# A gated recurrence with a softmax mixture layer behind it: order of the first loads, of a few sums, and of one group's queries

## The chip, the cores and the metric

The kernel runs on one core of a Trainium2 chip. A core has five engines that run side by side, each with its own queue of instructions: TensorE (PE in the profile; its weight loads are PEld), VectorE (DVE), ScalarE (ACT), GpSimd (POOL) and SyncE (SP), which here only issues transfers. They wait for each other through semaphores. Sixteen DMA engines move data between the chip's memory (HBM) and the core's own memory (SBUF); TensorE writes into a second small memory of banks (PSUM). The metric is the device time of one execution in microseconds (us); lower is better.

## What is computed

The inputs are q, k, v and alpha, float32 of shape (4 batches, 8 heads, 768 tokens, 48), and the weights w_in (384 x 1024), w_out (1024 x 384), which are float64, and a gain g_ln (1024).

```python
for t in range(S):                       # per batch and head
    state = alpha[:, :, t, :, None] * state + einsum('bhd,bhe->bhde', k[:, :, t], v[:, :, t])
    y[:, :, t] = einsum('bhd,bhde->bhe', q[:, :, t], state)
x = y.transpose(0, 2, 1, 3).reshape(B * S, H * D)          # 3072 x 384
h = x @ w_in                                               # 3072 x 1024
e = exp(h - max(h)); sm = e / (sum(e) + 1e-9)              # by row
solu = h * sm
ln = (solu - mean(solu)) / sqrt(var(solu) + 1e-6) * g_ln
out = ln @ w_out                                           # 3072 x 384
```

## The kernel before

**Groups.** The 768 tokens are cut into six groups of 128. A group holds those 128 tokens of all four batches, so 512 rows of the second part. The recurrence over a group is done in one piece, by cumulative products of alpha: keys are divided and queries multiplied by these products, scores between all pairs of tokens are taken on TensorE, masked to the lower triangle, and multiplied with v; a state is carried from group to group.

**Stages of a group's recurrence.** alpha, k and q must stand turned, with the 48 features of a head along partitions and tokens along the free side. The features of a head are split into 32 ("firsts") and 16 ("lasts"), so there are 12 blocks of 32 rows for 8 heads, held as three tiles of four blocks. Group 0 is turned on TensorE by multiplying with the identity (`turned`); later groups on DVE in part (`firsts`, `lasts`) or on TensorE. `scan_back` runs a product scan from the end of the group on DVE (L204), `inverses` and `scan_on` one from its beginning. Then k is multiplied into `kT`, q into `qv` (firsts) and `qe` (lasts). `apart` is a pair of ACT copies (L245) that spread `qe` over blocks, with `parity` deciding which rows are zero. `scores(g, half)` is 64 small matmuls (L278) for four heads: first those over the firsts of every head, then those over the lasts, which read what `apart` wrote. `masked` multiplies scores by the mask on DVE (L289), `read_values` multiplies them with v (L333), and y becomes x.

**Stages of the second part.** For each of eight column blocks `up` computes h = x w_in (L394), ACT takes the exponential `e` (L408), DVE multiplies h by e into `room` (L409), ACT squares that into `u` (L412), and running sums `p` over the column blocks are kept by DVE or POOL (L427). After that `down(n, half)` multiplies a batch's 128 rows by w_out (L507). The layer norm is applied after that product, by `finish(n)`, from sums over columns; `token_sums(g)` turns those sums so that they stand by token: a transpose into `cols` (L467) and three small DVE instructions, a copy into `sums` (L469), a square `sq` (L471) and `s` (L473). `finish` reads `s` and computes the row's scale on DVE, POOL and ACT.

**The weights.** w_in and w_out come as eight pieces of 64-bit numbers (`fetch`, L578), four of w_in (each 256 columns, three requests of 128 rows) and four of w_out; pieces 2 and 3 of w_in are fetched by the same three requests. Five DVE instructions a piece (`bits`) make float32 of them.

**Order.** The order of all instructions on each engine is written out by hand in the program's text. Group g's `up` is interleaved with group g+1's recurrence and group g-1's `down` by a plan: a table says for each of the eight column blocks what of the next group's recurrence is done ahead of it or behind it. Group 1 has a plan of its own (`first`), in which group 2's recurrence has lasts and firsts of the queries behind block 2, `apart` behind block 3, scores behind blocks 4 and 5. `firsts` transposes all eight heads in one DVE instruction (L179); POOL then multiplies them by the products of alpha in two instructions (`queries(0)` and `queries(1)`, L253).

**The start.** SP issues, in this order, alpha (two requests of two batches each), k, q, v and w_in; ACT issues the identity, the mask, `parity` and the gain, behind its first table load. Meanwhile TensorE does 14 matmuls of ones (`warm`, L452), then turns alpha, k and q. A transfer's completion is counted by one of eight semaphores in rotation, and a request waits until the one before it on its semaphore has landed.

The parts that are touched: `warm` (L449), `token_sums` (L454), the first loads (L667 to L689), the turning of alpha (L699 to L704), the multiplies of the queries with `apart` in them (L721), the order at L817 to L826, and "firsts" in `attend` (L882).

Of the kernel before, what the change touches and what calls it, by code (L numbers as in the profile page):

```python
# [32 lines left out]
def fast_path(ctx, tc, q, k, v, alpha, moe_w_in, moe_w_out, moe_g_ln, out):  # L33
# [105 lines left out]
    def by_token(x):  # L139

        return x.rearrange("p h u d -> p (h u d)").rearrange("p (b h d) -> p b h d", b=B, h=H)

    def load_first(src, dst, g):
        t = slice(g * P, (g + 1) * P)
        for b in range(0, B, 2):
            nc.sync.dma_start(
                out=by_token(dst)[:, b : b + 2].rearrange("p b h d -> p (b h) d"),
                in_=src[b : b + 2, :, t].rearrange("b h p d -> p (b h) d"),
            )

    def ends_of(src, tag=None):

        ends = ring.tile([P, T4], FP, name=tag) if isinstance(tag, str) else lots[tag][:, 0:T4]
        ends = ends.rearrange("p (b d) -> p b d", b=B)
        nc.scalar.copy(out=ends.rearrange("p b (h d) -> p b h d", h=H), in_=by_token(src)[:, :, :, E0:D])
        return ends

    def turned(src, ends, out, blocks=range(NB)):

        x = by_token(src)  # L160
        for j in blocks:
            for b in range(B):
                cols = x[:, b, j, 0:E0] if j < H else ends[:, b, E0 * (j - H) : E0 * (j - H) + E0]
                nc.tensor.matmul(
                    out[j // NP][32 * b : 32 * b + 32, j % NP], lhsT=cols, rhs=ident, start=True, stop=True,
                    tile_position=(0, 32 * b), skip_group_check=True,
                )
# [75 lines left out]
    def apart():  # L243
        for i in range(2):
            nc.scalar.mul(  # L245
                out=qv[:, H : 2 * H, 0:P].rearrange("p (j i) t -> p j i t", i=2)[:, :, i], in_=qe[:, :, 0:P],
                mul=parity[:, i : i + 1],
            )
# [22 lines left out]
    def scores(g, half, a=None):  # L271
        a = a or banks("a", [NP, P])
        for last in range(2):
            for i in (0, 2, 1, 3):
                h = half * NP + i
                kb, qb = (H + h // 2, H + h) if last else (h, h)
                for b in range(B):
                    nc.tensor.matmul(  # L278
                        a[b][:, i], lhsT=kT[quarter(b), kb], rhs=qv[quarter(b), qb, 0:P], start=not last and not i, stop=bool(last),
                        tile_position=(32 * b, 0), skip_group_check=True,  # L280
                    )
        masks[half] = a
# [163 lines left out]
                nc.scalar.copy(out=d["p"][:, i], in_=d["q"][i])  # L446
            d["unit"] = small_ones

    def warm(n, ps=ps_o, tag="o"):  # L449
        t = ps.tile([P, 512], FP, tag=tag, name="warm")  # L450
        for i in range(n):
            nc.tensor.matmul(t[:, 0:P], lhsT=ones, rhs=ones, start=True, stop=True)  # L452

    def token_sums(g):  # L454


        d = gr[g]
        t = ps_a.tile([P, B, 2, 32], FP, tag="a3", name="rows") if g else ps_h.tile([P, B, 2, 32], FP, tag="h", name="rows")
        for b in range(B):
            for r in range(4):  # L460
                c = b * P + 32 * r
                nc.tensor.matmul(
                    t[quarter(r), b], lhsT=d["unit"][:, 0:32], rhs=d["p"][:, :, c : c + 32], start=True, stop=True,
                    tile_position=(0, 32 * r), skip_group_check=True,
                )
        tt = work.tile([P, B, 2, 32], FP, name="cols")
        nc.vector.transpose(out=tt.rearrange("p b i t -> p (b i t)"), in_=t.rearrange("p b i t -> p (b i t)"))  # L467
        s = sums[:, g * B : g * B + B]
        nc.vector.tensor_copy(out=s[:, :, 1:3], in_=tt[:, :, :, 0])  # L469
        sq = small.tile([P, B], FP, name="sq")  # L470
        nc.vector.tensor_tensor(out=sq, in0=s[:, :, 1], in1=s[:, :, 1], op=ALU.mult)  # L471
        d["s"] = small.tile([P, B], FP, name="s")
        nc.vector.scalar_tensor_tensor(  # L473
            out=d["s"], in0=sq, scalar=1e-6 * DFF, in1=s[:, :, 2], op0=ALU.mult, op1=ALU.add
        )

    def last_norm():

# [88 lines left out]
    def fetch(i, slot, n=1):  # L567

        kind, f = pieces[i]
        w = n * F // (2 if kind else KC)  # L570
        raw = room[:, 1536 * slot : 1536 * (slot + n)].bitcast(U32).rearrange("p (c f w) -> p c f w", f=w, w=2)
        if kind:
            parts = [(slice(0, P), c, moe_w_out[(f + c) * P : (f + c + 1) * P, :]) for c in range(2)]
        else:
            parts = [(slice(0, P), c, moe_w_in[c * P : (c + 1) * P, f * P : f * P + w]) for c in range(KC)]
        for rows, c, src in parts:
            if float64:
                nc.sync.dma_start(out=raw[rows, c].rearrange("p f w -> p (f w)"), in_=src.bitcast(U32))  # L578
            else:
                dst = w_out[rows, f + c, 0:DM] if kind else w_in[rows, c, f * P : f * P + w]  # L580
                nc.sync.dma_start(out=dst, in_=src)
        for m in range(n):
            raws[i + m] = raw[:, :, w // n * m : w // n * (m + 1)]
# [81 lines left out]
    def inline(x, name):  # L665
        return nc.inline_tensor(np.ascontiguousarray(x, np.float32), name=name).ap()

    load_first(alpha, an, 0)
    nc.vector.memset(mone, -1.0)
    nc.scalar.activation(out=far[:, 0, 1:2], in_=mone, func=AF.Exp)  # L670
    nc.scalar.dma_start(out=ident, in_=inline(np.eye(P), "ident_c"))
    nc.scalar.dma_start(out=mask, in_=inline(np.triu(np.ones((P, P))), "mask_c"))
    odd = np.arange(P) // E1 % 2
    nc.scalar.dma_start(out=parity, in_=inline(np.stack([1 - odd, odd], 1), "parity_c"))
# [10 lines left out]
    nc.gpsimd.memset(kg, 0.0)  # L685
    load_v(0)
    fetch(0, 3)
    fetch(1, 4)
    fetch(2, 1, 2)  # L689
    nc.vector.memset(ones, 1.0)  # L690
    nc.vector.memset(small_ones, 1.0 / 32)
    nc.vector.memset(mhalf, -0.5)
# [3 lines left out]
        return [pool.tile([P, NP, P], FP, tag=tag, name=f"{name}{i}") for i, (pool, tag) in enumerate(where)]  # L696


    warm(14)  # L699
    t = three("tp_a", [(ps_a, "a0"), (ps_a, "a1"), (ps_a, "a2")])  # L700
    turned(an, ends_of(an, 1), t)
    for i in range(3):
        nc.scalar.copy(out=aT[:, NP * i : NP * i + NP, 1:SW], in_=t[i])  # L703
        scan_back(0, i)  # L704
    t = three("tp_k", [(ps_a, "a3"), (ps_h, "h"), (ps_h, "h")])
# [11 lines left out]
    for i in (0, 2, 1):  # L717
        if i == 1:
            scan_on(0, i)
        part = slice(NP * i, NP * i + NP)  # L720
        nc.vector.tensor_tensor(  # L721
            out=qe[:, :, 0:P] if i == 2 else qv[:, part, 0:P], in0=t[i], in1=aT[:, part, 1:SW], op=ALU.mult
        )
        if i == 2:
            apart()
    scores(0, 0)
    t = [x.tile([P, NP, P], FP, tag=n, name="a_" + n) for x, n in ((ps_h, "h"), (ps_o, "o")) for _ in range(2)]
    scores(0, 1, t)
# [92 lines left out]
    down(2, 1)  # L821
    scores(1, 1)
    masked(1)
    finish(0)
    finish(1)
    finish(2)  # L826
# [36 lines left out]
    def attend(a, what):  # L863

        more = a + 1 < G
        if what == "v":
            load_v(a)
        elif what == "keys":
            keys_T(a)
            keys(a)  # L870
            if more:
                load(k, kn, a + 1)
        elif what[:2] == "on":
            if what == "on2":
                inverses(a)
            scan_on(a, int(what[2]))
        elif what == "lasts":
            lasts(qn, qe[:, :, 0:P])
            ends_of_decay()
            queries(2)  # L880
            move_lasts()
        elif what == "firsts":  # L882
            firsts(qn, qv[:, 0:H, 0:P])
            queries(0)
            queries(1)
            move_firsts()
            if more:
                load(q, qn, a + 1)
        elif what == "apart":
            apart()  # L890
        elif what == "decay":
            decay(a)
        elif what == "keys_back":
            if more:
                keys_back(a)
        elif what[:6] == "scores":
            scores(a, int(what[6]))
        elif what[:6] == "masked":
            masked(int(what[6]))
        elif what == "alpha" and more:  # L900
            alpha_T(a + 1)
            if a > 2:
                attend(a, "over")
        elif what == "over" and more:
            alpha_over(a + 1)
            if a + 2 < G:
                load(alpha, an, a + 2)
        elif what == "back" and more:
            for i in range(3):
                scan_back(a + 1, i)  # L910
        elif what == "begin":
            read_begin()
        elif what[:4] == "read":
            read_state(int(what[4]))
        elif what == "values":
            read_values(a)
        elif what == "kv" and more and a != 4:
            next_state(a)
# [535 lines left out]
```

## Time and profile before

| | |
|---|---|
| time, median of 3 runs | 368.23 us (368.16 to 368.46) |
| the profiled execution's own time | 367.97 us |
| its span, first to last instruction | 366.2 us |
| granted TensorE clock | 1.000 |
| ACT and POOL busy | 146.4 us (40%) and 132.2 us (36%) |
| DMA, packets and bytes | 72871 packets, 36.06 MB |

The profile comes from one execution. A row of its timeline gives the start and the busy time (both us), the engine, the line, the operation with output and inputs, the tile shapes, how many instructions were put together in the row, and in brackets how long the engine was idle ahead of it and who released it. A row of the waits view gives engine, name and line that waited, who it waited for, and the total, the number and the longest of these waits. PEld rows are weight loads, which run beside matmuls.

The whole span in 40 slices of 9.2 us, each digit the busy share in tenths (9 is 90% or more):

```profile
PE   8899999999999999999999999999999999999994
DVE  0999989979998797936675935766946314345420
DMA  9995995326196409463035354004041000000011
```

The TensorE row is full from the third slice on. DVE is nearly full from the second slice to the sixteenth or so. The DMA engines are full for the first three slices.

### The profile page before, as it was taken

Reading aid. Unit: us, or ns where it says so; the run is one execution under the profiler, and the core shown is the slowest. Engines: PE = TensorE matmul, PEld = TensorE weight load, DVE = VectorE, ACT = ScalarE, POOL = GpSimd, SP = SyncE. Lnnn points to the kernel's source line nnn. Section 1 sums busy time; section 2 is a strip of 40 time slices with the busy share of each in tenths; the row PEclk is TensorE's granted clock in tenths of the full one; section 3 lists DMA queues with packets and bytes.
Section 4 is the critical chain, followed back from the end, with each engine's and each line's share of the span. In section 5 each row is a group of like instructions: output and inputs, shape, how many; then the busy total and the mean of one; then the engine's idle time right before and its main releaser. Section 6 shows DMA issues by size and latency. Waiting matters only on the chain. (4 is left out here: it accounts for less than half of the span.)

```text
span 366.2 us, 10036 instructions
## 1 busy us (share of the span) xinstructions
PE 357.8 (98%) x4341; PEld 215.0 (59%) x4341; DVE 245.0 (67%) x375; ACT 146.4 (40%) x260; POOL 132.2 (36%) x129
## 2 busy tenths in 40 slices
PE   8899999999999999999999999999999999999994
PEld 8784355666755566566575456475556565555552
DVE  0999989979998797936675935766946314345420
ACT  3647878182645262252521252431241132222110
POOL 7020000004449963774133764232773121233300
PEclk9999999999999999999999999999999999999999
DMA  9995995326196409463035354004041000000011
GB/s 180 183 338 152 204 309 124 88 67 159 50 234 141 109 21 180 85 152 94 21 92 112 83 121 126 3 25 88 21 107 55 0 25 0 24 21 22 23 47 51
DMA packets 72871, 36.06 MB, mean 98 GB/s; under 512 B 48232, under 2 KB 70000, under 8 KB 72816
## 3 DMA queue, kind: packets, MB, share of 16 engines
q1 hardware_dynamic: 71792, 34.39, 39.8%
q10 hardware_dynamic: 1024, 0.92, 0.8%
q8 instruction: 36, 0.59, 0.7%
q14 instruction: 19, 0.16, 0.2%
HBM read 25.30 MB, written 4.72 MB: 82 GB/s over the span
## 5 line engine op out<-in xcount | busy, mean ns | idle before, releaser
L507 PE MATMUL o<-w_out,room 128*128 128x385 f32 x384 | 134.0, 492 | 0.0
L394 PE MATMUL h<-x,w_in 128*128 128x512 f32 x288 | 131.7, 597 | 0.5 <-DVE g_col L642 0.5
L507 PEld LDWEIGHTS o<-w_out,room 128*128 128x128 f32 x384 | 71.0, 189 | 54.7 <-issue 13.1
L394 PEld LDWEIGHTS h<-x,w_in 128*128 128x128 f32 x288 | 53.2, 189 | 58.6 <-issue 48.5
L409 DVE TENSOR_TENSOR room<-h,e 128x512 f32<-128x512 f32 x40 | 27.5, 689 | 72.9 <-ACT e L408 72.9
L408 ACT ACTIVATE e<-h 128x512 f32<-128x512 f32 x40 | 24.0, 599 | 100.2 <-PE h L394 100.2
L427 POOL TENSOR_TENSOR p<-p,e 128x512 f32<-128x512 f32 x30 | 43.7, 1458 | 20.0 <-ACT e L408 19.9
L412 ACT ACTIVATE u<-room 128x512 f32<-128x512 f32 x40 | 25.2, 630 | 38.3 <-DVE room L409 38.3
L546 POOL TENSOR_TENSOR r<-sums,mhalf 128x1 f32<-128x1 f32 x20 | 14.8, 741 | 69.7 <-DVE sums L537 69.4
L289 DVE TENSOR_TENSOR sT<-a,mask 128x512 f32<-128x512 f32 x43 | 26.7, 681 | 8.0 <-PE a L278 7.9
L204 DVE TENSOR_TENSOR_SCAN hT<-aT,unit 128x516 f32<-128x516 f32 x18 | 24.4, 1399 | 7.6 <-ACT aT L703 7.5
L204 DVE TENSOR_TENSOR_SCAN aT<-aT,seed 128x516 f32<-128x516 f32 x18 | 27.4, 1551 | 0.2
L225 POOL TENSOR_TENSOR kT<-kT,hT 128x1024 f32<-128x1024 f32 (+1 forms) x8 | 14.2, 1800 | 32.7 <-DVE kT L179 32.7
L427 DVE TENSOR_TENSOR p<-p,u 128x512 f32<-128x512 f32 x30 | 22.5, 749 | 5.1 <-ACT u L412 5.1
L278 PEld LDWEIGHTS a<-qv,kT 32*128 32x128 f32 x704 | 21.4, 186 | 7.0 <-issue 2.6
L278 PE MATMUL a<-qv,kT 32*128 32x128 f32 x704 | 23.9, 278 | 0.4 <-POOL qv L253 0.3
L212 POOL COPY fend<-hT 128x12 f32<-128x12 f32 x6 | 3.1, 509 | 55.9 <-DVE hT L204 55.9
L333 PE MATMUL y<-sT,vn 128*32 128x128 f32 x768 | 22.6, 273 | 0.2 <-DVE sT L289 0.2
L333 PEld LDWEIGHTS y<-sT,vn 128*32 128x32 f32 x768 | 20.7, 110 | 1.6 <-issue 1.0
L196 ACT ACTIVATE sq<-an,mone 128x1536 uint8<-128x1536 f32 x12 | 18.9, 1572 | 0.2
L548 ACT ACTIVATE o_sb<-o,r 128x384 f32<-128x384 f32 x16 | 9.3, 582 | 18.5 <-POOL r L546 18.5
L261 POOL TENSOR_TENSOR state<-state,lot 128x384 f32<-128x384 f32 x10 | 8.8, 903 | 13.1 <-DMA lot<-qv 13.1
(148 smaller groups left out, 374.3 us busy)
## 6 DMA issues: line engine op xcount, KB each, us to landing
vn<-in_v_dram SPq DMA_DIRECT2D x24, 192.0 KB, 4.7
an<-in_alpha_dram SPq DMA_DIRECT2D x20, 192.0 KB, 4.1
out_dram<-o_sb SPq DMA_DIRECT2D x20, 192.0 KB, 1.9
room<-in_moe_w_out_dram SPq DMA_DIRECT2D x8, 384.0 KB, 5.5
kn<-in_k_dram SPq DMA_DIRECT2D x16, 192.0 KB, 5.6
qn<-in_q_dram SPq DMA_DIRECT2D x16, 192.0 KB, 4.1
lot<-qe SPq DMA_DIRECT2D x40, 64.5 KB, 2.1
lot<-qv SPq DMA_DIRECT2D x20, 129.0 KB, 2.4
```

Source lines behind the costliest of these rows:

```text
L196: nc.scalar.activation(out=sq, in_=x, func=AF.Relu, scale=sign, bias=mone, accum_out=over[:, g, i : i + 1])
L204: nc.vector.tensor_tensor_scan(out=o, data0=a, data1=s, initial=1.0, op0=ALU.mult, op1=ALU.add)
L278: nc.tensor.matmul(a[b][:, i], lhsT=kT[quarter(b), kb], rhs=qv[quarter(b), qb, 0:P], start=not last and not i, stop=bool(last), tile_posit ...
L289: nc.vector.tensor_tensor(out=sT[:, b, half * NP : half * NP + NP], in0=a[b], in1=mask[:, None, :].to_broadcast([P, NP, P]), op=ALU.mult,)
L333: nc.tensor.matmul(y_bank(b)[quarter(r), a], lhsT=lhsT, rhs=rhs, start=(b, r) not in begun, stop=stop, tile_position=(row, 32 * r), skip_g ...
L394: nc.tensor.matmul(h, lhsT=w_in[:, a, f * P : (f + 1) * P], rhs=d["x"][:, a].rearrange("p b t -> p (b t)"), start=(a == 0), stop=(a == KC ...
L408: nc.scalar.activation(out=e, in_=h, func=AF.Exp)
L409: nc.vector.tensor_tensor(out=u, in0=h, in1=e, op=ALU.mult)
L412: nc.scalar.activation(out=u2, in_=u, func=AF.Square)
L427: eng.tensor_tensor(out=p, in0=d[0][i] if f == 1 else p, in1=d[f][i], op=ALU.add)
L507: nc.tensor.matmul(d["o"][:, 0 : DM + 1], lhsT=u_of(g, f)[:, b * P : b * P + P], rhs=w_out[:, f], start=(f == 0), stop=(f == FC - 1), skip ...
L546: nc.gpsimd.tensor_tensor(out=r, in0=s[:, 3:4], in1=mhalf, op=ALU.pow)
```

## The change

**Start.** The identity is issued first on ACT. Alpha's first group is fetched by eight requests of 96 KB, heads 0 to 3 of the four batches and then heads 4 to 7, batches 0 and 1 from SP and 2 and 3 from ACT. The table load, mask, `parity` and gain come behind them on ACT. The first 14 warm matmuls are 92 x 92 instead of 128 x 128. TensorE turns alpha's first four blocks, the copy and the scan of that tile are issued, and then come the copy of the ends (`ends_of`, the lasts of all heads) and the other eight blocks.

**Weights.** Six of w_in's nine requests move from the start to the place behind group 0's `apart`. A small ACT copy into the place they write holds them until then.

**Sums.** The three small DVE instructions of `token_sums(0)` move from behind the transpose to just ahead of `finish(0)`.

**Queries.** For group 2 the transpose of the firsts and the multiplies are done in halves: four heads transposed, multiplied by POOL, then the other four.

```diff
-    def warm(n, ps=ps_o, tag="o"):
+    def warm(n, ps=ps_o, tag="o", w=P):
         t = ps.tile([P, 512], FP, tag=tag, name="warm")
         for i in range(n):
-            nc.tensor.matmul(t[:, 0:P], lhsT=ones, rhs=ones, start=True, stop=True)
+            nc.tensor.matmul(t[0:w, 0:w], lhsT=ones[:, 0:w], rhs=ones[:, 0:w], start=True, stop=True)
...
+        def rest():
+            nc.vector.tensor_copy(out=s[:, :, 1:3], in_=tt[:, :, :, 0])
+            sq = small.tile([P, B], FP, name="sq")
+            nc.vector.tensor_tensor(out=sq, in0=s[:, :, 1], in1=s[:, :, 1], op=ALU.mult)
+            d["s"] = small.tile([P, B], FP, name="s")
+            nc.vector.scalar_tensor_tensor(
+                out=d["s"], in0=sq, scalar=1e-6 * DFF, in1=s[:, :, 2], op0=ALU.mult, op1=ALU.add
+            )
+
+        if g:
+            rest()
+        else:
+            d["rest"] = rest
...
-    load_first(alpha, an, 0)
+    nc.scalar.dma_start(out=ident, in_=inline(np.eye(P), "ident_c"))
+    for h in (slice(0, NP), slice(NP, H)):
+        for b in range(B):
+            queue = nc.sync if b < 2 else nc.scalar
+            queue.dma_start(out=by_token(an)[:, b, h], in_=alpha[b, h, 0:P].rearrange("h p d -> p h d"))
     nc.vector.memset(mone, -1.0)
     nc.scalar.activation(out=far[:, 0, 1:2], in_=mone, func=AF.Exp)
-    nc.scalar.dma_start(out=ident, in_=inline(np.eye(P), "ident_c"))
...
     fetch(0, 3)
-    fetch(1, 4)
-    fetch(2, 1, 2)
...
-    warm(14)
+    warm(14, w=92)
     t = three("tp_a", [(ps_a, "a0"), (ps_a, "a1"), (ps_a, "a2")])
-    turned(an, ends_of(an, 1), t)
     for i in range(3):
+        if i == 0:
+            turned(an, None, t, range(NP))
+        elif i == 1:
+            turned(an, ends_of(an, 1), t, range(NP, NB))
         nc.scalar.copy(out=aT[:, NP * i : NP * i + NP, 1:SW], in_=t[i])
         scan_back(0, i)
...
         if i == 2:
             apart()
+            nc.scalar.copy(out=slots[4][:, 0:1], in_=parity[:, 0:1])
+            fetch(1, 4)
+            fetch(2, 1, 2)
...
     masked(1)
+    gr[0]["rest"]()
     finish(0)
...
         elif what == "firsts":
-            firsts(qn, qv[:, 0:H, 0:P])
-            queries(0)
-            queries(1)
+            for i, n in ((0, NP), (NP, NP)) if a == 2 else ((0, H),):
+                firsts(qn[:, i : i + n], qv[:, i : i + n, 0:P])
+                for j in range(i // NP, (i + n) // NP):
+                    queries(j)
             move_firsts()
```

## The prediction

> **What bounds the kernel now.** I read the page's busy times first, then the waits of PE, then the timeline around each wait, engine by engine.
>
> ```profile
> span 366.2 us, 10036 instructions
> PE 357.8 (98%) x4341; PEld 215.0 (59%) x4341; DVE 245.0 (67%) x375; ACT 146.4 (40%) x260; POOL 132.2 (36%) x129
> ```
>
> TensorE is busy for 98% of the span, so a gain must come from one of its few waits. The waits view lists them; these are all that reach 0.2 us.
>
> ```profile
> PE tp_k L164 <- DMA kn<-in_k_dram: 0.9, 1, 0.9
> PE h L394 <- DVE g_col L642: 0.5, 1, 0.5
> PE tp_a L164 <- DMA an<-in_alpha_dram: 0.3, 1, 0.3
> PE a L278 <- POOL qv L253: 0.3, 1, 0.3
> PE y L333 <- DVE sT L289: 0.2, 1, 0.2
> PE tp_q L164 <- DMA qn<-in_q_dram: 0.2, 1, 0.2
> ```
>
> All but the fourth lie before 29 us. The timeline of the start and of the two later places:
>
> ```profile
> 8.64 3.48 DVE L204 TENSOR_TENSOR_SCAN hT<-aT,unit 128x516 f32<-128x516 f32 x3 [7.54 <-ACT aT L703]
> 14.99 0.80 PEld L164 LDWEIGHTS tp_q<-ident,qn 128*32 128x32 f32 x28 [0.47 <-DMA qn<-in_q_dram]
> 17.35 0.68 DVE L721 TENSOR_TENSOR qe<-tp_q,aT 128x512 f32<-128x512 f32 x1
> 18.07 1.34 ACT L245 ACTIVATE qv<-qe,parity 128x512 f32<-128x512 f32 x2 [2.42 <-DVE qe L721]
> ...
> 78.50 1.65 PEld L278 LDWEIGHTS a<-qv,kT 32*128 32x128 f32 x56 [0.34 <-DVE qv L811]
> 80.41 0.69 DVE L289 TENSOR_TENSOR sT<-a,mask 128x512 f32<-128x512 f32 x1 [1.97 <-PE a L278]
> ...
> 109.55 2.05 DVE L179 STREAM_TRANSPOSE qv<-qn 128x1024 f32<-128x1024 f32 x1
> 111.43 0.69 DVE L427 TENSOR_TENSOR p<-p,u 128x512 f32<-128x512 f32 x1
> 111.68 2.44 POOL L253 TENSOR_TENSOR qv<-qv,aT 128x512 f32<-128x512 f32 x2 [0.81 <-DVE qv L179]
> 113.12 2.26 PE L278 MATMUL a<-qv,kT 32*128 32x128 f32 x64 [0.26 <-POOL qv L253]
> 113.28 1.32 ACT L245 ACTIVATE qv<-qe,parity 128x512 f32<-128x512 f32 x2
> 113.41 1.25 DVE L427 TENSOR_TENSOR p<-p,u 128x512 f32<-128x512 f32 x1 [0.69 <-ACT u L412]
> ```
>
> Three stages matter. (1) To 20 us: DVE's first scan waits 7.54 us for alpha, and from there DVE runs almost without a gap to 78.45. (2) At 78 us PE waits about half a microsecond (its previous matmul ends at 77.98, the next weight load of this group is at 78.50) for DVE's last multiply (L811, 77.76 to 78.45), which frees the bank that scores(1,0) writes. (3) At 113 us PE finishes group 1's h at 112.71 and waits to 113.12 for POOL's query multiply. From scores(2,0)'s end at 115.3 I see no PE wait that these edits could touch.
>
> **Two rules of the Trainium skill.** "SBUF — State Buffer", section "SBUF: two separate sides", says that DVE and GpSimd share a port pair as an exclusive lock for a whole instruction, which a DVE operation with two SBUF inputs contends for. The trace agrees: `p` (L427) takes 0.69 us at 111.43, but 1.25 at 113.41, where it ends 0.54 us after POOL's multiply does (114.12). The forecast goes by these rows. "DMA: Bandwidth & Descriptors", section "Issuing engines are not separate DMA queues", says that the queues of SP and ACT share the same 16 engines. Here the 192-byte packets of alpha, k and q moved some 220 KB per us with the DMA engines solidly busy from 2 to 11 us: the trace does not contradict it, so two issuing engines should not bring q in earlier.
>
> **Part 1: identity first, alpha by halves.** Bytes stay the same; 8 requests replace 2. Alpha landed at 4.64 (batches 0,1) and 6.79; heads 0 to 3 of all batches should now land near 4.4. The 14 warm matmuls shrink from 5.11 us to (92/128) of it at best on the columns, 3.7; as the first ones run at the slow rate (0.213 us per record till 4.6, then 0.112), I take their end as 5.2 rather than 6.12. Then 16 turns (half of some 1.8 us), the copy (0.59) and handing over give a first scan at about 7.0 instead of 8.64. Three scans of 1.16 start-to-start need the second alpha half (6.8, then turns and a copy: 8.4), so they end at 10.7 rather than 12.12: DVE 1.4 earlier. But the q transfer, behind the same bytes, still lets PE turn q only at 14.99. The first q tile is ready at 16.0, the third (needed for `qe`) at 16.9. Before, DVE reached `qe` late (17.35) because it was behind; now it waits for PE and starts about 17.0. So of 1.4 us only 0.35 survives. `apart` (1.34, zero idle behind it) follows, then scores(0,0), which needs it for its last half: end 20.02 becomes 19.66. Its own unhindered length, 1.79 from 17.73, would end at 19.52, so the cap is 0.5 unless q itself lands earlier. Masks, y, the w_in conversion and the first h (28.39, after DVE's 28.24) follow on DVE without a gap, so they shift too: **-0.36**. What the trace doesn't show is q's landing under the new order: the eight requests use up the rotating completion semaphores, so k must be issued after a first quarter has landed (about 4.4, while alpha still occupies the engines till 6.8: hidden) and q after a last one. Bounds: +0.3 (k or q held, or a cold clock after a shorter warm-up) to -1.0 (q 0.6 earlier).
>
> **Part 2: six w_in requests behind `apart`.** They move from SP's 17.9 to 21.15 to about 19.1 to 22. SP now waits on an ACT copy of 128 elements (0.2, behind which stands ACT's score copy at 20.33, itself idle 0.92 before). Pieces 1 to 3 landed by 25.5 and 29.54 and are converted from 27.3 and 31.3: some 1.5 us of cover. Piece 0 (landed 23.52, needed 23.91 before, 23.55 now) is ahead in the queue. **0**, between -0.1 and +0.3 if piece 0 or 1 slips.
>
> **Part 3: three DVE instructions later.** `rest` costs start to start 63.16 to 63.65, 0.49. DVE is without a gap from there to 78.45, so scores(1,0)'s bank comes free 0.49 earlier: PE -0.5 at 78.5. At 80.41 DVE waits for PE again, so the chain behind starts 0.5 earlier also. At 88.0 the same 0.49 is put in before finish(0), into a DVE stretch with no idle from 80.41 to 112.7 but 0.34 at 105.08, which comes from DVE's own sums through POOL and ACT and so moves along. PE, 0.5 ahead, meets DVE again at scores(2,0): its last half waits for `apart` (two ACT copies, ends 113.99 and 114.61; PE's next starts at 114.04 and 114.66: no slack), `apart` for `u`, this for DVE's room (ends 112.71), which stands in that chain. So **-0.03**: gained at 78, given back at 115. Bounds -0.5 (idle inside DVE takes it) to +0.5.
>
> **Part 4: third queries by halves.** The transpose's halves take 0.98 start to start, 1.16 each (row of 128x512 at 65.64). POOL's first multiply starts at about 110.8 and, at 1.09 alone, ends at 111.87. That releases PE's wait for it (0.4), but scores(2,0) ends with `apart`, so nothing comes of that. DVE's `p`, due at 111.5, now meets a running POOL instruction; by the row at 113.41 it ends 0.55 after POOL, 112.42 instead of 112.12. room, u, `apart` and the end of scores(2,0) are that much later: **+0.30**. Below: -0.1 (the lock spares it; `apart` gates anyway). Above: +1.4, if POOL's second multiply is let in ahead of `p` (1.09 more); before, the two alternated.
>
> **Sum:** -0.36 + 0 - 0.03 + 0.30 = -0.09 us. The profiled execution took 367.97 (span 366.2 and 1.8 around it), so 367.88; the median is 0.26 above that execution, hence 368.14, said as 368.1.
>
> **Rivals.**
> - *Faster.* q lands earlier because kn and qn are no longer interleaved with mask and gain requests, or DVE after 80 us has more give than I read. Then -0.7 at the start, or -0.5 of stage 2 stays; with +0.3 or 0 at part 4 the sum is -0.6 to -1.3; at its centre 367.3. For: all first-stage waits are for DMA or DVE, and both are relieved. Against: bytes and packet size are unchanged.
> - *Slower: the port lock.* POOL takes both halves before `p`: +1.4 in place of 0.30, sum +1.0, 369.2. It decides from the point where the second transpose half signals POOL (111.69 + 0.1) before the first multiply ends (111.87), which my own figures just allow; against it, the alternation seen before.
> - *The transfers swallow the start.* DVE waits 0.4 for w_out at 49.5. If that stream doesn't move up, DVE alone keeps the old time, and with stage 2's release the PE wait returns as 0.34: sum about +0.3, 368.5, inside "no change".
> - *It doesn't do what it says.* The halves of part 4 aim at the query wait, but `apart` ends the stage; that is in the forecast.
>
> **Numbers.** Measurement can tell about 0.2% (0.74 us) from nothing. Forecast with the third rival 0.43; faster 0.36; slower 0.21 (port lock 0.13, a held k, q or w_in transfer 0.08). The likeliest case's own range is 367.6 to 368.8; with the two sides' centres the range becomes 366.9 to 369.1.
>
> **What would show it.** First scan at 7.0 (8.64); q's turn still at 14.99; scores(0,0)'s end at 19.66; first h at 28.0; no PE wait at 78; `p` near 111.5 lengthened to about 0.9 to 1.1; the end of scores(2,0) at 115.2. Wrong if q lands over 0.4 earlier or later, if the DVE chain from 80 to 112 shows idle that absorbs 0.5, or if `p` waits for two POOL multiplies.

## The result, and the profile after

The changed kernel is slower: 369.63 us median (368.52 to 370.81, 11 runs) against 368.14 us (367.66 to 368.80, 11 runs) of the kernel before in the same set. The ratio is 1.0042 with a 95% interval of 1.0033 to 1.0052, so +1.5 us, outside the forecast range. The single runs also spread twice as far as those of before.

The profiled execution took 368.77 us, one of the faster ones. Page, then TensorE's waits up to 120 us:

```profile
span 367.0 us, 10048 instructions
PE 358.2 (98%) x4341; PEld 214.6 (58%) x4341; DVE 245.6 (67%) x376; ACT 146.2 (40%) x261; POOL 130.8 (36%) x129
```

```profile
PE tp_k L164 <- DMA kn<-in_k_dram: 1.2, 1, 1.2
PE warm L452 <- DVE ones L697: 1.1, 1, 1.1
PE a L278 <- ACT qv L245: 0.7, 1, 0.7
PE y L333 <- issue: 0.3, 1, 0.3
PE y L333 <- DVE sT L289: 0.2, 1, 0.2
```

The waits for POOL's query at 113 us and for `g_col` at 28 us are gone. Two are new: one for `apart` (ACT qv L245), and one with no releaser ("issue"), in which TensorE waits for nothing that the profile shows. The timeline rows that answer to those of before:

```profile
7.80 3.48 DVE L204 TENSOR_TENSOR_SCAN hT<-aT,unit 128x516 f32<-128x516 f32 x3 [6.70 <-ACT aT L713]
14.94 0.80 PEld L164 LDWEIGHTS tp_q<-ident,qn 128*32 128x32 f32 x28 [0.17 <-DMA qn<-in_q_dram]
16.93 0.69 DVE L731 TENSOR_TENSOR qe<-tp_q,aT 128x512 f32<-128x512 f32 x1 [0.18 <-PE tp_q L164]
17.65 1.34 ACT L245 ACTIVATE qv<-qe,parity 128x512 f32<-128x512 f32 x2 [2.06 <-DVE qe L731]
23.34 3.04 PE L333 MATMUL y<-sT,vn 128*32 128x128 f32 x102 [0.26 <-issue]
...
77.78 1.88 PEld L278 LDWEIGHTS a<-qv,kT 32*128 32x128 f32 x64 [0.55 <-DVE qv L824]
...
109.44 2.07 DVE L179 STREAM_TRANSPOSE qv<-qn 128x512 f32<-128x512 f32 x2
111.33 1.04 DVE L427 TENSOR_TENSOR p<-p,u 128x512 f32<-128x512 f32 x1
110.74 2.58 POOL L253 TENSOR_TENSOR qv<-qv,aT 128x512 f32<-128x512 f32 x2
112.39 1.17 PE L278 MATMUL a<-qv,kT 32*128 32x128 f32 x32
114.30 1.34 PE L278 MATMUL a<-qv,kT 32*128 32x128 f32 x32 [0.73 <-ACT qv L245]
```

q is turned at 14.94 and `qe` made at 16.93, as forecast. At 78 us the weight loads run through (64 in one row); before, the group broke at 78.50. At 111 us `p` takes 1.04 us, and scores(2,0), which could start at 112.39, breaks off in its middle until `apart` is done at 114.30.

Set against each other matmul by matmul, the two traces run like this (us, after minus before at the same instruction):

| place | before | after | difference |
|---|---|---|---|
| first h | 28.39 | 27.95 | -0.44 |
| h's third column block starts | 35.31 | 35.22 | -0.09 |
| first matmul behind scores(1,0) | 80.49 | 79.78 | -0.71 |
| scores(2,0) starts | 113.12 | 112.39 | -0.73 |
| first matmul behind scores(2,0) | 115.32 | 115.57 | +0.26 |
| span | 366.2 | 367.0 | +0.8 |

At their own places parts 1, 3 and 4 read as forecast in this trace. The start's gain, however, is gone between 28 and 35 us, where the forecast saw nothing. Behind 115 us another 0.24 is lost in y at 296 us and 0.3 in the last store. This execution lies 0.86 below the median: what the others lose isn't in it.

### The profile page after: what moved, and what is told of

The parts are those of the page before. It is cut to its first block, busy times and chain, and to the rows that moved or that the text cites. A ratio compares the mean times of both kernels' runs of the same rounds, so it can differ in the third digit from the quotient of the medians.

```text
span 367.0 us, 10048 instructions
## 1 busy us (share of the span) xinstructions
PE 358.2 (98%) x4341; PEld 214.6 (58%) x4341; DVE 245.6 (67%) x376; ACT 146.2 (40%) x261; POOL 130.8 (36%) x129
## 5 line engine op out<-in xcount | busy, mean ns | idle before, releaser
L427 POOL TENSOR_TENSOR p<-p,e 128x512 f32<-128x512 f32 x30 | 42.2, 1405 | 20.0 <-ACT e L408 19.9
L427 DVE TENSOR_TENSOR p<-p,u 128x512 f32<-128x512 f32 x30 | 23.7, 790 | 5.2 <-ACT u L412 5.2
L333 PE MATMUL y<-sT,vn 128*32 128x128 f32 x768 | 23.4, 274 | 0.5 <-issue 0.3
L333 PEld LDWEIGHTS y<-sT,vn 128*32 128x32 f32 x768 | 20.9, 110 | 2.4 <-issue 1.7
```

Source lines behind the costliest of these rows:

```text
L333: nc.tensor.matmul(y_bank(b)[quarter(r), a], lhsT=lhsT, rhs=rhs, start=(b, r) not in begun, stop=stop, tile_position=(row, 32 * r), skip_g ...
L427: eng.tensor_tensor(out=p, in0=d[0][i] if f == 1 else p, in1=d[f][i], op=ALU.add)
```

## The experiments

Every set carried the kernel before along; its median was 367.98 to 368.08. Theory A stands for the port pair at 111 us, B for an unsteady start. C (TensorE's instruction supply) came from the first four traces. D is a cost in parts 1 or 3 that no trace had shown, E a wait of TensorE for w_in's data or for a bank.

### One part undone at a time

Each takes one part of the change back to the text of before, all else as changed. For the queries, as an example:

```diff
-            for i, n in ((0, NP), (NP, NP)) if a == 2 else ((0, H),):
+            for i, n in ((0, H),):
```

> Everything of the change but the queries by halves. Theory A (the port pair at 111 us: POOL's second multiply holds back DVE, and the half-way copies and the end of scores(2,0) with it): the loss is gone, 368.0 us, 0.1 below the kernel before, and the runs lie as close together as those of before (about 1 us). Theory B (the start: transfers or TensorE's instruction supply under the new order of requests vary from run to run): still about +1.1 us over before, with runs spread over 2 us.

> Everything but the identity and alpha by halves and the smaller warm-up. Theory A: still slower than before by 1.0 to 1.6 us, since the loss lies at 113 us and what the start gains is mostly spent by then. Theory B: 0 to +0.5 us over before, runs close together.

> Everything but the deferral of six w_in requests. Theory A: as the changed kernel, +1.2 to +1.6 us. Theory B, if the late w_in requests are the disturbance: 0 to +0.5 us; if alpha's are: +1.5 us.

> Everything but the move of the three small DVE instructions. Theories A and B: PE's wait at 78 us is back (0.4 us) but DVE is 0.5 us earlier at 112 us, so the time is that of the changed kernel within 0.3 us, +1.2 to +1.8 over before.

| undone | median (runs) | ratio to before, 95% |
|---|---|---|
| queries by halves | 369.09 (367.68 to 372.47) | 1.0027 (1.0013 to 1.0041) |
| alpha by halves | 369.29 (368.20 to 372.00) | 1.0033 (1.0021 to 1.0046) |
| w_in later | 368.81 (367.94 to 369.74) | 1.0017 (1.0009 to 1.0025) |
| sums later | 368.83 (367.73 to 372.97) | 1.0026 (1.0010 to 1.0042) |

A alone falls: without the halves the kernel stays 1.1 us slower. B's culprit isn't alpha. Without the deferral 0.6 to 0.8 us are left (0 to 0.5 expected under B), so it isn't the deferral alone either. What stands out is the spread: the three kernels that keep the late w_in requests have runs up to 372 and 373, the one without them ends at 369.74. TensorE's waits up to 45 us with the sums undone (this profiled execution took 372.97):

```profile
PE h L394 <- issue: 2.3, 1, 2.3
PE tp_k L164 <- DMA kn<-in_k_dram: 1.6, 1, 1.6
...
PE y L333 <- issue: 0.9, 1, 0.9
...
PE kv L371 <- issue: 0.3, 1, 0.3
```

Three waits "for nothing" add up to 3.5 us. The trace tells what they are. On a queue of their own, transfers of 16,384 bytes run all through the kernel, 36 in each trace:

```profile
q8 instruction: 36, 0.59, 0.7%
```

The breaks stand at TensorE's 961st, 1217th and 1473rd instruction in every one of these traces: 256 apart, so one transfer per block of 256 instructions at 64 bytes each. These are the fetch times from the traces' DMA records, and what TensorE did at the block's edge:

| kernel of the trace | 3rd fetch | goes on | idle there | 4th fetch | goes on | idle there | 5th fetch | goes on | idle there |
|---|---|---|---|---|---|---|---|---|---|
| before | 20.99-21.93 | 23.25 | 0 | 27.46-28.45 | 31.18 | 0 | 32.44-33.36 | 34.88 | 0 |
| changed | 20.91-21.85 | 23.34 | 0.5 | 27.83-28.80 | 30.73 | 0 | 32.31-33.23 | 34.68 | 0.24 |
| w_in undone | 21.15-22.09 | 23.37 | 0.6 | 27.69-28.69 | 30.85 | 0 | 32.53-33.45 | 34.80 | 0.24 |
| alpha undone | 21.80-22.75 | 24.23 | 1.1 | 29.36-30.33 | 31.84 | 0.4 | 34.99-36.05 | 37.49 | 1.9 |
| halves undone | 21.79-22.73 | 24.21 | 1.3 | 29.86-30.84 | 32.27 | 0.7 | 35.27-36.22 | 37.65 | 1.6 |
| sums undone | 21.59-22.53 | 23.94 | 1.2 | 29.43-30.41 | 31.78 | 0.5 | 35.41-36.63 | 37.98 | 2.5 |

(Idle: the gap between two starts less the usual one.) Wherever TensorE waited at an edge it went on 1.28 to 1.51 us after the fetch had ended. In this trace of the kernel before the fifth block came just in time: 1.52 us. In the changed kernel's the start puts TensorE 0.44 ahead and the fetch comes only 0.13 earlier, so TensorE waits again: between these two traces that is where the start's gain went. Fetch times scatter from run to run: in a second trace of the kernel before (below) the fifth began at 30.64 and cost nothing. The 0.24 lost in y at 296 us stands at such an edge too, the 8129th instruction (28 blocks behind the 961st): its fetch ended at 294.88 and it starts 1.3 us later.

In the traces with alpha, halves or sums undone ACT, and in two of them DVE, also waited for w_in's data, by 0.3 to 0.8 us at 24 and 32 us. But near 35 us ACT waits for TensorE's h and DVE for ACT, while TensorE has no releaser.

Why are the fetches late? The view by stretches of time (start and end of the stretch, its length, busy time of five engines, clock, DMA share, GB/s), first of the kernel before:

```profile
22.00:26.00 4.00, 3.80 (x130) 3.49 (x128) 3.91 (x7) 2.04 (x4) 1.63 (x3) 1.00 1.01 376
26.00:30.00 4.00, 3.54 (x28) 2.34 (x20) 3.79 (x7) 3.30 (x8) 0.00 (x0) 1.00 0.43 172
```

and with the sums undone:

```profile
22.00:26.00 4.00, 2.86 (x93) 2.44 (x93) 3.20 (x6) 1.29 (x3) 1.33 (x2) 1.00 0.96 254
26.00:30.00 4.00, 4.00 (x53) 2.94 (x45) 3.79 (x6) 3.15 (x7) 0.00 (x0) 1.00 0.72 288
```

The w_in stream has moved: 376 GB/s from 22 to 26 us became 254, and 172 from 26 to 30 became 288. The fourth fetch begins in both near the end of this stream (last packets at 28.35 and 31.35), at 27.46 and at 29.43. The fifth follows 5 to 6 us later; with the sums undone the first of group 1's loads, in 192-byte packets from 33.68 us on, are then ahead of it, and in the microsecond before 35.41 no other data moves. In the kernel before these packets start at 33.00, behind the fifth fetch. This is theory C: the late requests of w_in delay TensorE's instructions. The changed kernel's own trace has nearly the same rates (250 and 284) and its fourth fetch at 27.83, so the fetch can come late when the stream has moved, but need not.

### One part alone

> The kernel before with the deferral of six w_in requests alone. Theory C (the deferred requests bring TensorE's own instruction fetches, which the trace shows as 16 KB transfers, late: TensorE runs out of instructions near 35 us): median +0.6 to +1.3 us over before, single runs up to +4, and in a slow profiled run a TensorE wait without a releaser (issue) of over 1 us between 34 and 38 us. Theory A (only the port pair at 111 us costs): within 0.2 us of before.

> The kernel before with the identity and alpha by halves and the smaller warm-up alone. Theory C: the first h comes 0.4 us earlier than in the kernel before, but near 34.7 us TensorE must wait for the same instruction fetch (its fetch ends near 33.2 us and TensorE goes on some 1.4 us later), so that at 44 us it is level: the time within 0.2 us of before. The forecast's own step: -0.36 us, 367.65.

> Parts 1 and 3 together, w_in's requests and the queries as before. Theories A and C: TensorE reaches 112 us 0.6 to 0.7 us earlier than before and waits that much longer for POOL's queries; the time within 0.2 us of before, runs within 1.2 us of each other. Rival D (a cost in part 1 or 3 that no trace here has shown): +0.4 us or more.

> The kernel before with the queries by halves alone. Theory A: DVE's p near 111.5 us is held by POOL to about 1.0 us instead of 0.69, the end of scores(2,0) comes 0.3 to 0.5 later, time +0.3 to +0.5 us. If A is wrong: -0.3 to 0.

| kernel | median (runs) | ratio to before, 95% |
|---|---|---|
| w_in later alone | 369.84 (367.98 to 372.19) | 1.0049 (1.0025 to 1.0074) |
| alpha by halves alone | 368.13 (367.60 to 370.45) | 1.0007 (0.9995 to 1.0018) |
| alpha and sums | 368.56 (367.67 to 369.37) | 1.0010 (1.0001 to 1.0019) |
| queries by halves alone | 368.44 (367.94 to 369.50) | 1.0012 (1.0006 to 1.0019) |

The deferral alone makes a loss as large as the whole (expected up to +1.3, measured +1.8 in seven runs, interval 0.9 to 2.7). Its profiled execution was its fastest, so the wait of over a microsecond isn't in that trace. Alpha alone brings nothing that can be told: its first h came not 0.4 earlier but 1.4 us later in the profiled run, because the third fetch came at 22.95 and y stood idle for 2.0 us at that block's edge. A wait at an edge was expected, but at the fifth block's.

Alpha and sums cost 0.4, where 0.2 at most was expected: rival D is right that something was missing. The trace (of 369.01 us) shows it:

```profile
PE y L333 <- issue: 1.3, 1, 1.3
PE a L278 <- POOL qv L253: 0.8, 1, 0.8
```

The third fetch came at 22.12, so TensorE reached its first h 0.66 later than in the kernel before, and the wait that the sums take away at 78 us only brought it level (+0.04). The three DVE instructions, done later, then lengthen DVE's way (28.67 us from 80.62 to the `qe` transpose, 28.18 before), and scores(2,0) starts 0.68 later. In this trace, then, part 3 costs: it is neutral only where TensorE isn't late already.

The halves alone cost 0.44, as theory A has it:

```profile
111.39 1.04 DVE L427 TENSOR_TENSOR p<-p,u 128x512 f32<-128x512 f32 x1
112.35 0.68 DVE L409 TENSOR_TENSOR room<-h,e 128x512 f32<-128x512 f32 x1
113.73 1.42 DVE L427 TENSOR_TENSOR p<-p,u 128x512 f32<-128x512 f32 x1 [0.70 <-ACT u L412]
```

`p` takes 1.04 instead of 0.69, as in the changed kernel, and `room` and all behind it shift by 0.33.

### The block edges moved

If instructions run short, then dummy instructions far ahead must matter: 16 fewer warm instructions move every edge 16 instructions later in the work. Each warm matmul counts as four instructions (two loads, two multiplies).

```diff
-    warm(14, w=92)
+    warm(10)
```

The other way it is `warm(18, w=72)`; before_again is the kernel before, unchanged.

> The changed kernel with 10 warm matmuls of 128 x 128 in place of 14 of 92 x 92: 16 TensorE instructions fewer ahead of everything, and about the same time for them. Theory C (instruction supply): every edge between two fetched blocks falls 16 instructions later in the work, which between 34 and 38 us are eight matmuls of 0.43 us; the wait there shrinks from 1.5 to 2.5 us to under 0.7, and the median falls by 0.6 to 1.3 us to 368.3 to 369.0. Rival E (TensorE waits there for w_in data or a bank): no change, 369.0 to 369.9.

> The changed kernel with 18 warm matmuls of 72 x 72: 16 TensorE instructions more ahead of everything, so every edge between fetched blocks falls 16 instructions earlier in the work. Theory C: TensorE meets the edge of its fifth block some 2 us earlier, while the fetch comes no sooner: waits of 2 to 4 us between 31 and 37 us, median 370.3 to 371.8. Rival E: 369.0 to 369.9.

> The kernel before once more, for a second trace of it. Theory C: TensorE goes on at its 961st, 1217th and 1473rd instruction (256 apart, 16 KB of 64 bytes) no earlier than 1.35 us after the end of the third, fourth and fifth instruction fetch, and waits there by less than 0.5 us; time 368.0 within 0.6.

> The kernel before with the identity and alpha by halves alone, and 10 warm matmuls of 128 x 128. Theory C: the edges fall 16 instructions later, so the start's gain of 0.3 to 0.4 us outlasts 44 us: 367.5 to 367.8, faster than before. Rival E: as with 14 of 92 x 92, 368.1.

With 16 instructions fewer the changed kernel falls to 368.53 us (1.0014, 1.0006 to 1.0023), with 16 more it rises to 374.73 (371.01 to 377.91; 1.0141, 1.0105 to 1.0177 without the highest run), for warm matmuls that take 4.63 and 4.37 us (4.60 in the changed kernel). That decides for C against E; the second went beyond what was expected. TensorE's waits of that kernel from 20 to 200 us, those above 0.2:

```profile
PE o L513 <- issue: 1.8, 1, 1.8
PE kv L371 <- issue: 1.5, 1, 1.5
PE a L278 <- ACT qv L245: 0.9, 1, 0.9
PE h L394 <- issue: 0.5, 1, 0.5
```

The fifth edge now falls into kv (the state update behind h's first block), where instructions are short, and a later edge, at its 4545th instruction (14 blocks behind the 961st), costs 1.8 us more near 144 us. With 10 the wait at h is gone; 0.8 us at y stays, as the third edge moved only among y's short matmuls. The second trace of the kernel before has idle time of 0.72 at the third edge too (under 0.5 expected), yet its first h comes at 28.46 (28.39): there DVE's w_in conversion, which ends near 28.2 in both, hides it. It ran 367.92 us, as expected. Alpha alone with 10 warm matmuls gave 368.18 us, 1.0005 (0.9994 to 1.0017; 367.5 to 367.8 expected): lowest run 367.20, but half of the runs above 368.3. No gain is shown. Its trace, of 367.46 us, has the third fetch at 20.27 and no idle time at the edge; alpha alone's, of 369.24 us, had it at 22.95.

Last, the edges moved by 44 instructions, with 3 warm matmuls of 128 x 512:

```diff
-                nc.tensor.matmul(t[0:w, 0:w], lhsT=ones[:, 0:w], rhs=ones[:, 0:w], start=True, stop=True)
+                nc.tensor.matmul(t[:, 0 : P * w].rearrange("p (r c) -> p r c", c=P), lhsT=ones,
+                                 rhs=ones[:, None, :].to_broadcast([P, w, P]), start=True, stop=True)
...
-    warm(14, w=92)
+    warm(3, w=4)
```

> The changed kernel with 3 warm matmuls of 128 x 512 in place of 14 of 92 x 92: about the same time, 44 TensorE instructions fewer, so every edge between fetched blocks falls 44 instructions later in the work (the fifth's near 43 us instead of 34). Theory C: no wait for instructions is left between 20 and 43 us but up to 0.5 us in y; what remains is part 4's cost less the start's gain: 368.0 to 368.4, runs within 1 us of each other. If the deferral costs in another way: 369 or more.

> The identity and alpha by halves alone, with 3 warm matmuls of 128 x 512. Theory C: the start's gain of 0.35 to 0.45 us reaches the end in nearly every run: 367.5 to 367.7, and no second group of runs above 368.3 as with 10 warm matmuls. If the start doesn't gain even with instructions at hand: 368.0 and more.

The changed kernel fell as expected, to 368.40 us (1.0012, 1.0004 to 1.0020; the runs 1.6 us apart where 1 was expected), with no idle time left at the three edges, though its warm-up took 5.49 us. Alpha alone did the opposite of what was expected: 369.15 us (367.72 to 371.57; 1.0029, 1.0017 to 1.0041). Its trace, of the run of 367.83 us, has the third fetch at 22.49 and 1.3 us of idle time in y. In the traces with w_in's requests early the third fetch began anywhere from 20.3 to 23.0 us, in those with the deferral from 20.9 to 21.8, with the two behind it later. Its runs above 369 us have no trace, and what they lose stays open.

### The stage at 113 us

Is it `apart` that ends scores(2,0)? It was moved ahead of the exponential of block 3:

```diff
-        head={3: "keys_back"},
+        head={3: "keys_back apart"},
...
-            0: "v", 1: "on1", 2: "lasts firsts", 3: "apart", 4: "scores0 masked0", 5: "scores1 masked1 decay",
+            0: "v", 1: "on1", 2: "lasts firsts", 4: "scores0 masked0", 5: "scores1 masked1 decay",
```

> The kernel before with group 2's apart issued behind keys_back of block 3 and ahead of that block's exponential on ACT, instead of behind its square. Theory A (the end of scores(2,0) is set by apart, not by the queries): apart ends near 112.2 us instead of 114.6, scores(2,0) starts as before, runs its own 1.8 us and ends 0.3 to 0.4 us earlier: 367.6 to 367.8. If apart does not set it: no change, or +0.3 by the later exponential.

> The same with the queries by halves. Theory A: with apart out of the way the half-way query is what scores(2,0) needs; it starts when TensorE arrives (112.7), ends by 114.6, 0.7 to 0.8 us before the kernel before: 367.2 to 367.5, so part 4 turns from a cost of 0.4 us to a gain of 0.3 over the whole-query kernel. If the port pair itself is the cost: 367.8 to 368.2, no better than with whole queries.

> Parts 1, 3 and 4, w_in's requests as before, 10 warm matmuls of 128 x 128, apart ahead of the exponential. Theories A and C together: start -0.3, 78 us -0.4 (no longer given back, since DVE's chain ends in apart no more), 113 us -0.4: 366.9 to 367.3, below both kernels. If another wait takes the place: 367.6 to 368.0.

> Parts 1 and 3 with 10 warm matmuls of 128 x 128 in place of 14 of 92 x 92. Theory C (edges 16 instructions later): 0.3 to 0.6 us below parts 1 and 3 with 92 x 92, 367.6 to 368.0, with the gain of part 3 still given back at 113 us.

Measured with `apart` early: 368.60 us (1.0019, 1.0008 to 1.0031) with whole queries, 368.12 (1.0005, 0.9997 to 1.0014) with halves, and 368.61 (1.0013, 1.0003 to 1.0023) with parts 1, 3 and 4 and 10 warm matmuls. Parts 1 and 3 with 10 warm matmuls, `apart` as before, gave 368.17 (1.0009, 0.9998 to 1.0019). With 14 the ratio was 1.0010, so the gain of 0.3 to 0.6 us that was expected from the edges isn't shown, though the medians lie 0.4 apart. From the end of scores(1,0) to that of scores(2,0) it was 34.83 us before, 34.76 with the early `apart` alone, 35.24 with halves alone, and 34.36 with both. So with the halves `apart` did end the stage, and with it out of the way they gain. With whole queries its removal brings 0.07 and not the 0.3 to 0.4 expected: POOL's second multiply, which ends at 114.19, holds the weight loads there. And the wait moved on. With `apart` early the exponential and with it the masks come later, and scores(2,1) is what stretches:

```profile
113.08 2.07 PE L278 MATMUL a<-qv,kT 32*128 32x128 f32 x64
115.08 2.84 PE L394 MATMUL h<-x,w_in 128*128 128x512 f32 x6
117.85 2.69 PE L278 MATMUL a<-qv,kT 32*128 32x128 f32 x64
```

In this kernel (halves, `apart` early) the first score group of 64 takes 2.07 and the second 2.69. What was gained at 115 us is lost by 121. The time of the whole-query version is no measure of this stage alone: its trace also has 1.1 us of idle time at the third edge, and that of parts 1, 3 and 4 has 1.6. The expected 366.9 to 367.3 was missed, and so was 367.6 to 368.0, expected if another wait took the place; no version ran clearly below the kernel before.

## Why the prediction was wrong

- **Part 2 failed, and with it the forecast.** "0, between -0.1 and +0.3 if piece 0 or 1 slips" looked only at those who wait for w_in's data. It left out what else is fetched at that time: TensorE's own instructions, whose fourth and fifth blocks came up to 2.4 and 3.0 us later than in the first trace of the kernel before. Deferral alone measured +1.8 us (interval 0.9 to 2.7). The changed kernel loses 0.9 us less with its edges 16 instructions later (+0.55 over its set's median instead of +1.49). How the stream holds up a fetch is not shown. For the data itself the step held in the changed kernel's trace; where pieces slipped, in the traces with parts undone, DVE and ACT waited up to 0.8 us, and TensorE's waits show none for it. The hint was in the trace of before, in 16 KB transfers at 27.46 and 32.44 and TensorE going on 1.52 us after the second; only its named waits were read, and this one was just hidden.
- **Part 1**: -0.36 was right at its place in the changed kernel's trace (-0.44 at the first h; `qe` at 16.93 for 17.0; q at 14.94 for 14.99). The first scan came at 7.80 instead of 7.0, since the warm-up ended at 5.7 and not 5.2; this cost nothing. That the gain would "follow on DVE without a gap" to the end was wrong: TensorE met an instruction block that came hardly sooner. Where w_in's requests stay early even the gain at the first h is not sure: alone, part 1 showed none (1.0007, 0.9995 to 1.0018).
- **Part 3**: right for the changed kernel's trace. Gained 0.62 at 78 us for 0.5; DVE's way from 80 to its `qe` transpose at 108.6 grew from 28.18 to 28.62 us, 0.44 for 0.49; given back at 115. That it needs TensorE on time at 78 us was not seen.
- **Part 4**: right in mechanism and size. `p` 1.04 (0.9 to 1.1), cost +0.36 in the trace (DVE's `room` ahead of it stood at -0.10, the end of scores(2,0) at +0.26) and +0.44 (0.2 to 0.7) alone, for +0.30. POOL's second multiply was not let in first. Here the Trainium skill's rule agrees with the trace: "SBUF — State Buffer", "SBUF: two separate sides", has the pair locked for a whole instruction, and `p` ended 0.54 us after POOL's first multiply (111.83), while POOL's second took 1.54 us instead of 1.09.
- **The slower rival** stood on the wrong mechanism: the port lock cost 0.4, not 1.4; that its centre of 369.2 lies near the measured time is luck. In the numbers: of +1.5 us, 0.9 goes away with the edges and 0.4 is part 4; the last 0.2 is not assigned.
- **Two readings of the trace of before** were off and cost nothing: the list of TensorE's waits leaves out 1.1 us ahead of the first warm matmul, and w_in's pieces 1 and 2 are first read at 28.23 and 31.73, not at 27.3 and 31.3, so their cover was larger than written.

## What to carry to other kernels

A transfer's cost is not only when its data is needed but what else is being fetched then, an engine's own instructions included. Where an engine runs hundreds of short instructions while big loads stream, look at the instruction fetches, and at how closely the engine follows them. Waits marked "issue" a fixed number of instructions apart (256 here) point to such a shortage, and dummy instructions added or removed far ahead test it. Before halving a step to start its consumer earlier, find what ends that consumer.

## What the runs showed of the hardware

TensorE's instructions come in 16 KB blocks of 256 while it runs: 36 transfers in each of the twenty traces. One took 0.9 to 2.7 us (in the traces of the kernel before 0.9 to 1.7). In traces with the deferral the fourth began at 27.8 to 29.9 us, without it at 26.8 to 28.2; the fifth at 32.3 to 35.4 with it, and at 30.4 to 34.2 without. When a fetch is asked for is not in the trace, so how long it was queued can't be told.

A shortage can cost a second time. With the sums undone, TensorE's break near 36 us was followed by a stretch at half clock (the view by stretches as above, the clock third from the end):

```profile
36.00:39.00 3.00, 1.02 (x3) 0.54 (x4) 0.66 (x1) 0.28 (x1) 0.00 (x0) 1.00 0.85 160
39.00:43.00 4.00, 4.00 (x7) 1.68 (x6) 2.42 (x3) 1.72 (x5) 0.00 (x0) 0.57 0.92 197
43.00:47.00 4.00, 4.00 (x10) 1.71 (x9) 3.31 (x5) 3.88 (x8) 0.00 (x0) 1.00 0.65 147
```

It lasted 3.41 us, during which a matmul of h took 0.85 us from start to start instead of 0.43, by estimate about 1.7 us lost. With 18 warm matmuls the same came after the break near 144 us. The Trainium skill's "TensorE: Matmul & The Clock Gate", "Part 1: The HAM clock gate", gives windows of some 3.4 us after which an idle TensorE falls to half rate. The stretch has that length, but the breaks ahead of it were shorter than a window (2.9 us from one start to the next here, 2.3 near 144 us); breaks of 2.4 and 2.1 us at the fifth edge, with alpha and with the halves undone, were not followed by it.
